# Expert weights loaded into tiles that the attention leaves, a third buffer of bucket rows, and the first experts' rows turned on TensorE

## The chip, the core and the metric

The kernel runs on one core of a Trainium2 chip. The metric is the device time of one execution in microseconds (us), median of several runs. Of the engines, PE is TensorE (matmuls), DVE is VectorE, ACT is ScalarE, POOL is GpSimd, and SP is SyncE, which here only issues DMAs. DMAs issued by SP stand in the profile under queue q1 (hardware_dynamic), those issued by POOL under q0 (software_dynamic); 16 DMA engines work for both.

## What is computed

Blockwise causal attention over 8 batches, 8 heads, 576 positions, 64 channels; its output, as 4608 rows of 512, goes through a noisy top-2 router and a mixture of 8 experts (512 to 1024 to 512, ReLU between).

```python
scores = np.where(mask, scale * q @ k^T, -1e9); attn = softmax(scores); x = (attn @ v) as (4608, 512)
noisy = x @ w_gate + log1p(exp(x @ w_noise)) * noise
top2 = the two largest of noisy per row; top2_w = softmax over these two
for e in range(8):
    for k in range(2):
        mask = top2[:, k] == e
        h = np.maximum(x[mask] @ w1[e], 0.0)
        out[mask] += top2_w[mask, k, None] * (h @ w2[e])
```

## The kernel before

**Stages.** The batches go in four groups of two (g = 0 to 3, 1152 rows each). For each group POOL loads q, k and v, PE turns q and k into `qT` and `kT`, computes scores, ACT takes the exponentials into `esc` (two buffers, one per half of the heads), PE multiplies by v (`vt`), DVE divides and writes the rows into `xr`. Then the router: PE turns the rows of `xr` (five pieces; their copies out of PSUM land in three buffers `xT0` to `xT2`), computes the logits from them (`logits`, L596), and DVE makes slots. POOL scatters the rows by `slots` into a bucketed DRAM tensor `xd` (18 indirect DMAs for each group, `scatter`, L707).

**Buckets.** Groups 0 and 1 form half 0, groups 2 and 3 half 1. In each half each expert has a bucket of 640 rows: 16 buckets, b = 0 to 15, where b is half times 8 plus expert. For a bucket SP loads the rows with a transposing DMA from `xd` into `xg` (`load_x`, L840; two buffers `xg0`, `xg1`); PE runs layer 1 (`layer1`, L898, matmul at L906: 64 matmuls of 128x320), ACT the ReLU into `h` (L912), PE layer 2 (`layer2`, L916, matmul at L922: five row tiles of eight matmuls of 128x512). The result rows go through `y` tiles to the DRAM tensor `yd` (`store_row`, L935, on SP). Buckets 0 and 1 are cut finer: pieces of 256, 256 and 128 rows, of which the first needs group 0's scatters alone; part of them is worked on between the attention of group 3. In the second half POOL gathers from `yd` (L945), DVE sums (L958, L980), and the rows are stored to the output.

**Weights.** Each expert has four pieces, W1 in two and W2 in two (`load_w`, L815), cast from float32 to bfloat16 by DMAs that POOL issues. Experts 0 and 1 have tiles of their own. Expert 7 lies where the raw q and k lay. Experts 2 to 6 lie in a pool `late`, opened where the attention's tiles lay, and their loads depend on the end of the whole attention (`att_done`).

**What sets the order.** A planner (`Plan`) gives each operation a name, engine costs, a due time, and resources that it takes and frees (buffers, PSUM banks); it simulates and writes the instructions of each engine out in the order that results. The engines work in order. `DUE` spaces the buckets' due times from 150. Operations added with `anchor=True` (weights among them) also wait, on the chip, for the last exponential or ReLU on ACT that stands before them in the plan. Names: `LX` is a load of bucket rows, `F1` and `F2` the layers, `RE` the ReLU, `YS` the store to `yd`, `W1`/`W2` weights, `D3.j` the scatters of group 3.

## Time and profile before

| | us |
|---|---|
| median of three runs (480.6 to 489.99) | 485.77 |
| profiled execution, device time | 478.8 |
| its span, first to last instruction | 477.0 |
| PE busy in the span | 411.8 (86%) |
| ACT busy | 258.9 (54%) |
| POOL busy | 258.6 (54%) |
| DVE busy | 160.2 (34%) |
| q0 (POOL's DMAs), share of 16 engines | 65.7% |
| q1 (SP's DMAs), share of 16 engines | 27.2% |
| mean granted clock of PE | 0.95 |

The profile is of one execution. Its busy shares are averages over stages of different kinds: the attention lasts to about 165 us, the buckets from then to the end. A timeline row gives an instruction's start and how long it took; in square brackets stands the idle time of its engine just ahead of it and what ended it. A row of SP's queue gives the time in which SP was busy issuing, not the transfer. The clock of PE is given as a share of full speed.

### The profile page before, as it was taken

The page shows a single profiled execution, that of the slowest core. Times are in us where ns is not written, and L with a number is a line of the kernel's source. Part 1 is how long each engine was busy: PE and PEld are TensorE (multiplying, and loading weights), DVE is VectorE, ACT ScalarE, POOL GpSimd, SP SyncE. Part 2 cuts the span into 40 slices and gives each one's busy share as a digit, 9 for nine tenths or more (in the row PEclk, how much of TensorE's full clock was granted, in tenths as well). Part 3 has the DMA queues.
Part 4 walks back from the last instruction along what each step waited for, and adds up shares of the span by engine and source line. Part 5 has one row for each costly group of instructions (what it writes and reads, how often), then busy time and mean ns, then how long its engine had stood idle before and what let it go on. Part 6 is the DMA issues. An engine that isn't in the chain of part 4 may idle for free. (4 is left out here: it accounts for less than half of the span.)

```text
span 477.0 us, 10736 instructions
## 1 busy us (share of the span) xinstructions
PE 411.8 (86%) x4308; PEld 262.6 (55%) x4344; DVE 160.2 (34%) x428; ACT 258.9 (54%) x448; POOL 258.6 (54%) x293
## 2 busy tenths in 40 slices
PE   3889999878699898599996989999989939999990
PEld 2567767667466775356553555555545525555550
DVE  4748788774733440000000020002432313233221
ACT  1778789854667644255542445466545524556520
POOL 7756458785874782743211000027577757577764
PEclk9979999996889999799998999999999978999997
DMA  9999999999969789959999993238856494875532
GB/s 122 185 201 188 182 180 153 196 182 173 159 140 192 213 160 227 238 135 201 211 186 221 184 172 97 56 84 163 269 125 166 131 146 133 206 189 184 187 104 90
DMA packets 131945, 80.26 MB, mean 168 GB/s; under 512 B 90848, under 2 KB 119853, under 8 KB 131888
## 3 DMA queue, kind: packets, MB, share of 16 engines
q0 software_dynamic: 69856, 52.37, 65.7%
q1 hardware_dynamic: 62032, 27.14, 27.2%
q8 instruction: 36, 0.59, 0.5%
q14 instruction: 21, 0.17, 0.1%
HBM read 71.43 MB, written 35.17 MB: 223 GB/s over the span
## 5 line engine op out<-in xcount | busy, mean ns | idle before, releaser
L906 PEld LDWEIGHTS <-w 128*128 128x128 bf16 x1088 | 105.3, 100 | 74.0 <-issue 28.5
L495 ACT ACTIVATE esc<-sc 128x1024 bf16<-128x1024 f32 x96 | 93.1, 1027 | 25.4 <-PE sc L476 24.7
L922 PEld LDWEIGHTS <-h 128*128 128x128 bf16 x640 | 62.1, 98 | 68.6 <-issue 2.5
L906 PE MATMUL sc<-xg,w 128*128 128x320 bf16 (+2 forms) x544 | 83.9, 294 | 16.6 <-DVE xr L958 7.4
L711 POOL DMA_INDIRECT xd<-xr,slots x72 | 71.7, 996 | 43.8 <-issue 16.4
L906 PE MATMUL bk<-xg,w 128*128 128x320 bf16 (+1 forms) x544 | 88.2, 303 | 7.1 <-DMA xg<-xd 7.1
L922 PE MATMUL bk<-w,h 128*128 128x512 bf16 x350 | 88.7, 382 | 1.8 <-ACT h L912 0.5
L912 ACT ACTIVATE h<-sc 128x320 bf16<-128x320 f32 (+1 forms) x120 | 50.7, 447 | 47.4 <-PE sc L906 34.9
L945 POOL DMA_INDIRECT xr<-yd,slots x36 | 36.6, 1017 | 67.9 <-DMA yd<-xr 56.9
L912 ACT ACTIVATE h<-bk 128x320 bf16<-128x320 f32 (+1 forms) x124 | 55.7, 453 | 31.4 <-PE bk L906 24.6
L922 PE MATMUL sc<-w,h 128*128 128x512 bf16 x254 | 64.8, 379 | 1.0 <-DVE xr L958 0.4
L469 PE MATMUL sc<-qT,kT 64*128 64x512 bf16 (+4 forms) x320 | 39.8, 313 | 7.4 <-ACT esc L495 5.9
L945 POOL DMA_INDIRECT xr<-yd,grow x35 | 35.9, 1026 | 13.2 <-issue 9.8
L873 DVE TENSOR_TENSOR rtmp<-rc,rowid 128x40 f32<-128x40 f32 x1 | 0.2, 225 | 105.6 <-DMA rc<-xd 105.6
L537 PEld LDWEIGHTS <-esc 128*128 128x128 bf16 x640 | 24.0, 100 | 8.9 <-issue 7.2
L556 DVE TENSOR_TENSOR xr<-bk,rden 128x256 bf16<-128x256 f32 x66 | 28.0, 424 | 2.3
L819 POOL DMA_DIRECT2D w<-in_moe_w_dram x16 | 12.4, 781 | 29.0 <-ACT h L912 28.3
L537 PE MATMUL bk<-vt,esc 128*128 128x65 bf16 x584 | 26.4, 198 | 1.7 <-DVE xr L556 0.8
L416 DVE COPY kT<-bk 128x1024 bf16<-128x1024 bf16 (+1 forms) x24 | 24.9, 1039 | 7.1 <-PE bk L395 6.1
L469 PEld LDWEIGHTS <-kT 64*128 64x128 bf16 x320 | 15.5, 97 | 18.8 <-issue 9.7
L964 POOL DMA_INDIRECT out_dram<-xr,trow x17 | 17.3, 1015 | 15.3 <-DVE xr L958 12.3
L476 PE MATMUL sc<-ones_mat,maskA 64*128 64x64 bf16 x256 | 23.6, 197 | 0.8 <-issue 0.8
(164 smaller groups left out, 415.1 us busy)
## 6 DMA issues: line engine op xcount, KB each, us to landing
w<-in_moe_w_dram POOLq DMA_DIRECT2D x32, 512.0 KB
yd<-xr SPq DMA_DIRECT2D x45, 128.0 KB
rq<-in_q_dram POOLq DMA_DIRECT2D x16, 256.0 KB
rk<-in_k_dram POOLq DMA_DIRECT2D x16, 256.0 KB
vt<-in_v_dram POOLq DMA_DIRECT2D x16, 256.0 KB
yd<-y SPq DMA_DIRECT2D x30, 128.0 KB
out_dram<-o SPq DMA_DIRECT2D x18, 128.0 KB
out_dram<-xr SPq DMA_DIRECT2D x18, 128.0 KB
```

What stands on the lines that cost most here:

```text
L416: nc.vector.tensor_copy(o, i)
L469: nc.tensor.matmul(out=sc[:, hf, off:off + z - a], lhsT=kT[sl, c0 + jt * P:c0 + jt * P + P], rhs=qT[sl, c0 + a:c0 + z], start=True, stop=n ...
L476: nc.tensor.matmul(out=sc[:, hf, off:off + 64], lhsT=maskA[sl, :], rhs=ones_mat[sl, 0:64], start=False, stop=True, skip_group_check=True)
L495: return nc.scalar.activation(out=esc_t[i][:, hh, :, piece * 512:(piece + 1) * 512], in_=sc, func=AF.Exp, scale=scale)
L537: nc.tensor.matmul(out=a[:, hh, :], lhsT=esc[:, hh, hf, c:c + P], rhs=vb[:, jt, hf, h, 0:D + 1], start=(jt == 0), stop=(jt == ib))
L556: nc.vector.tensor_tensor(out=xr[:, idx, st * SET * D:(st + 1) * SET * D].rearrange("p (h d) -> p h d", h=SET), in0=a[:, :, 0:D], in1=rden ...
L711: ins = nc.gpsimd.indirect_dma_start(out=xd[half].bitcast(I32), out_offset=bass.IndirectOffsetOnAxis(ap=slots[:, g * TG + idx, i:i + 1], a ...
L906: nc.tensor.matmul(out=hp[:, j * n:(j + 1) * n], lhsT=w1sb[:, db, fb * P:(fb + 1) * P], rhs=xg[:, db, c0:c0 + n], start=(db == 0), stop=(d ...
L912: return nc.scalar.activation(out=h_t[pl.slot(("h", b))][:, s * nb:(s + 1) * nb, c0:c0 + n], in_=bank(("hp", b, i, s))[:, 0:nb * n].rearra ...
L922: nc.tensor.matmul(out=yp, lhsT=h[:, fb, c * P:(c + 1) * P], rhs=w2sb[:, fb, :], start=(fb == 0), stop=(fb == FB - 1))
L945: ins = nc.gpsimd.indirect_dma_start(out=g_t[pl.slot(key)], out_offset=None, in_=yd[half][0:len(es) * CAP, :], in_offset=bass.IndirectOffs ...
L964: ins = nc.gpsimd.indirect_dma_start(out=out, out_offset=bass.IndirectOffsetOnAxis(ap=trow[:, e, c:c + 1], axis=0), in_=out_tile(("o", b, ...
```

## The change

- `NX` stays at two `xg` buffers, and the three `xT` buffers become one tile, whose memory is a third `xg` buffer once the last logits (`G3.0` to `G3.4`) are read.
- The buckets' due times start at 135, not 150.
- The pool `late` goes. Expert 2 lies where the raw q and k lay; experts 3 and 4 in `esc0` and `esc1`; expert 5 in `vt0` and `vt1`; expert 6 in `qT` and `kT`; expert 7 in the rest of `esc0` and `esc1`. Each load depends on those parts of the attention that read that tile last (`freed`), and the weights are issued in the order of the experts.
- The rows of buckets 0 and 1 are loaded in tiles of 128 rows with plain DMAs into `y` tiles (`load_tile`); PE turns each with four transposes into a PSUM bank (`XT`), and DVE or ACT copies it into `xg` (`XX`). There are two more `y` tiles, one of them the tile `zero`, after its use.
- The scatters of group 3 have a later due time (190).

```diff
-    NG_, NY, NO, NX = 0, 3, 0, 2
+    NG_, NY, NO, NX = 0, 4, 0, 2
-    xT_t = [low.tile([P, 2, DB, P], BF16, name=f"xT{i}") for i in range(3)]
+    xT_all = low.tile([P, 3, 2, DB, P], BF16, name="xT")
+    xT_t = [xT_all[:, i] for i in range(3)]
...
+    xg_t.append(xT_all.rearrange("p a b c d -> p (a b c d)")[:, 0:DB * CAP].rearrange("p (b n) -> p b n", b=DB))
+    zero = consts.tile([P, DR], BF16)
+    y_t += [zero[:, 0:Dm]]
+    pl.resource("y", 1, float("inf"))
...
-                   deps=[f"R{g}.rows", f"R{g}.w1", f"R{g}.tok", f"Z{half}"], due=r1 + 7 + j * 0.9 - 0.,
+                   due=(r1 + 7 - 0. if g < NG - 1 else 190.) + j * 0.9,
...
-    DUE, t_ = {}, 150.
+    DUE, t_ = {}, 135.
-    W1 = {0: ("low", 0), 1: ("low", 1), E - 1: ("rgt", 0)}
-    for e in range(2, E - 1):
-        W1[e] = ("late", e - 2)
...
     def w_of(e, which):
+        if e < EARLY:
+            return (w1_t if which == 1 else w2_t)[e]
+        if e == EARLY:
+            return rgt2()["w1" if which == 1 else "w2"]
+        esc = [esc_t[pl.slot(("esc", last, st))].rearrange("p a b c -> p (a b c)") for st in range(2)]
+        if e < EARLY + 3:
+            return view(esc[e - EARLY - 1], which - 1, which)
+        if e == EARLY + 3:
+            return view(vt[pl.slot(("vt", last - 2 + which))].rearrange("p j b h d -> p (j b h d)"), 0, which)
+        if e == EARLY + 4:
+            return view(qT if which == 1 else kT, 0, which)
+        return view(esc[which - 1], 2, which)
+
+    def freed(e, which):
+        av_done = [[f"A{last}.{st}.{i}" for i in range(TG)] for st in range(2)]
+        if e < EARLY:
+            return []
+        if e == EARLY:
+            return raw_done
+        if e < EARLY + 3:
+            return av_done[e - EARLY - 1]
+        if e == EARLY + 3:
+            return [f"A{last - 1}.{st}.{i}" for st in range(2) for i in range(TG)] if which == 1 else av_done[0] + av_done[1]
+        if e == EARLY + 4:
+            return [f"Q{last}.{u}" for u in range(UG)]
+        return av_done[which - 1]
...
-    w_rel = {0: 60., 1: 100.}
+    w_rel = {0: 60., 1: 100., 2: 140.}
...
+    def load_tile(b, c):
+        half, e = SEQ[b]
+        r = e * CAP + c * P
+        ins = nc.sync.dma_start(out=y_t[pl.slot(("xl", b, c))], in_=xd[half][r:r + P, 0:Dm])
+        return rows_landed(ins, half, groups(b, c // 2))
+
+    def turn_tile(b, c):
+        tp = bank(("xp", b, c)).bitcast(BF16)
+        for db in range(DB):
+            nc.tensor.transpose(tp[:, db * P:(db + 1) * P], y_t[pl.slot(("xl", b, c))][:, db * P:(db + 1) * P], ident)
+
+    def tile_turned(b, c, eng):
+        o = xg_of(b)[:, :, c * P:(c + 1) * P]
+        if eng == "DVE":
+            nc.vector.tensor_copy(o, tp)
+        else:
+            nc.scalar.activation(out=o, in_=tp, func=AF.Copy)
...
+    grant("zeros", ["Z0", "Z1"], (("y", NY, NY + 1),))
+    pl.resource("xg", 1, float("inf"))
+    grant("logits", [f"G{NG - 1}.{j}" for j in range(5)], (("xg", NX, NX + 1),))
```

The order of the instructions changes in two places above all. On SP, before the change, from the load of the last 256 rows of bucket 1 that wait for group 1 (`xg1`) to the load of bucket 4 (the second `xg0` of 640 rows):

```order
L844 DMA_TRANSPOSE xg1_112<-xd0 128x4x256
L938 DMA yd0<-y0_115 128x512
L844 DMA_TRANSPOSE xg1_112<-xd0 128x4x128
L938 DMA yd0<-y1_116 128x512
L938 DMA yd0<-y2_117 128x512
L938 DMA yd0<-y0_115 128x512
L938 DMA yd0<-y1_116 128x512
L938 DMA yd0<-y2_117 128x512
L844 DMA_TRANSPOSE xg0_111<-xd0 128x4x640
L938 DMA yd0<-xr0_106 128x512 x3
L844 DMA_TRANSPOSE xg1_112<-xd0 128x4x640
L938 DMA yd0<-xr0_106 128x512 x2
```

After the change, on SP, from the last but one plain load of bucket 1 (`y2`) to the load of bucket 4 (`xg1`):

```order
L868 DMA y2_115<-xd0 128x512
L868 DMA y3_116<-xd0 128x512
L860 DMA_TRANSPOSE xT_108<-xd0 128x4x640
L975 DMA yd0<-zero_159 128x512
L975 DMA yd0<-y0_113 128x512
L868 DMA y2_115<-xd0 128x512
L975 DMA yd0<-y1_114 128x512
L975 DMA yd0<-xr0_106 128x512 x3
L860 DMA_TRANSPOSE xg0_109<-xd0 128x4x640
L975 DMA yd0<-xr0_106 128x512 x2
L975 DMA yd0<-zero_159 128x512
L860 DMA_TRANSPOSE xg1_110<-xd0 128x4x640
```

The load of bucket 2 stood behind six stores of buckets 0 and 1 and went into `xg0`; it now stands ahead of all of them and goes into `xT`. The loads of buckets 3 and 4 go into `xg0` and `xg1`.

On POOL, before the change, from the scatters of group 2 (`xd1` from `xr0`) past those of group 3 (`xr1`):

```order
L711 DMA xd1<-xr0_106,slots_101 9728x260 x18
L817 DMA w1_2_3612<-in_moe_w1_dram 128x2x1024 x2
L819 DMA w2_2_3617<-in_moe_w2_dram 128x4x512 x2
L817 DMA w1_3_3613<-in_moe_w1_dram 128x2x1024 x2
L711 DMA xd1<-xr1_107,slots_101 9728x260 x18
L819 DMA w2_3_3618<-in_moe_w2_dram 128x4x512 x2
L817 DMA w1_4_3614<-in_moe_w1_dram 128x2x1024 x2
```

After the change, on POOL, the same place:

```order
L716 DMA xd1<-xr0_106,slots_101 9728x260 x18
L836 DMA w1_2_3617<-in_moe_w1_dram 128x2x1024 x2
L838 DMA w2_2_3618<-in_moe_w2_dram 128x4x512 x2
L836 DMA esc0_139<-in_moe_w1_dram 128x2x1024 x2
L838 DMA esc0_139<-in_moe_w2_dram 128x4x512 x2
L836 DMA esc1_140<-in_moe_w1_dram 128x2x1024 x2
L838 DMA esc1_140<-in_moe_w2_dram 128x4x512 x2
L716 DMA xd1<-xr1_107,slots_101 9728x260 x12
L836 DMA vt0_143<-in_moe_w1_dram 128x2x1024
L716 DMA xd1<-xr1_107,slots_101 9728x260 x2
```

Six weight pieces stood between the scatters of groups 2 and 3; now twelve stand there, and the last scatters of group 3 are mixed with the pieces of expert 5.

## Rows read from the trace of the kernel before

**Rows 1.** Timeline of PE: start, us, engine, line, op, tiles, shape, count [idle before].

```profile
196.12 1.23 PE L906 MATMUL bk<-xg,w 128*128 128x320 bf16 x4 [7.13 <-DMA xg<-xd]
197.14 1.27 PE L906 MATMUL sc<-xg,w 128*128 128x320 bf16 x4
198.20 2.30 PE L906 MATMUL bk<-xg,w 128*128 128x320 bf16 x8
200.34 1.79 PE L906 MATMUL sc<-xg,w 128*128 128x320 bf16 x12
...
255.15 1.23 PE L906 MATMUL sc<-xg,w 128*128 128x320 bf16 x4 [5.42 <-DMA xg<-xd]
...
258.66 0.71 PE L906 MATMUL sc<-xg,w 128*128 128x320 bf16 x4
...
275.73 0.70 PE L906 MATMUL sc<-xg,w 128*128 128x320 bf16 x4 [1.54 <-DMA xg<-xd]
...
293.20 0.71 PE L906 MATMUL sc<-xg,w 128*128 128x320 bf16 x4
...
311.13 0.71 PE L906 MATMUL sc<-xg,w 128*128 128x320 bf16 x4
...
392.90 1.23 PE L906 MATMUL sc<-xg,w 128*128 128x320 bf16 x4 [7.37 <-DVE xr L958]
```

**Rows 2.** Timeline of PE around the router of group 3 and after it.

```profile
164.53 0.39 PE L582 MATMUL bk<-ident,xr 128*128 128x128 bf16 x4
164.76 1.03 PE L922 MATMUL sc<-w,h 128*128 128x512 bf16 x4
165.62 0.45 PE L600 MATMUL sc<-wgn,xT 128*128 128x16 bf16 x12
...
174.39 2.82 PE L906 MATMUL sc<-xg,w 128*128 128x128 bf16 x40
```

**Rows 3.** Timeline of SP's queue: loads of buckets 2, 4, 5 and 6.

```profile
176.37 15.12 SPq L844 DMA_TRANSPOSE xg<-xd  x1
...
210.50 2.39 SPq L844 DMA_TRANSPOSE xg<-xd  x1
...
227.83 13.41 SPq L844 DMA_TRANSPOSE xg<-xd  x1
...
247.80 21.11 SPq L844 DMA_TRANSPOSE xg<-xd  x1
```

**Rows 4.** DMA queues from 212 to 216 us: packets, MB, share of 16 engines.

```profile
q1 hardware_dynamic: 2488, 0.64, 72.2%
```

**Rows 5.** DMA queues from 232 to 255 us.

```profile
q0 software_dynamic: 2707, 3.71, 92.0%
q1 hardware_dynamic: 2686, 0.75, 26.4%
```

**Rows 6.** Stretches: us, busy PE, PEld, DVE, ACT, POOL; clock, DMA share, GB/s.

```profile
164.00:168.00 4.00, 3.95 (x52) 2.92 (x51) 1.82 (x6) 1.75 (x6) 3.08 (x4) 1.00 0.44 152
...
196.00:200.00 4.00, 3.88 (x15) 2.22 (x15) 0.00 (x0) 1.30 (x3) 3.09 (x4) 0.50 1.51 308
...
208.00:212.00 4.00, 4.00 (x27) 2.44 (x25) 0.00 (x0) 2.40 (x6) 0.76 (x1) 1.00 0.03 7
...
236.00:240.00 4.00, 3.95 (x22) 2.08 (x22) 0.00 (x0) 1.59 (x4) 0.74 (x1) 1.00 1.15 201
```

**Rows 7.** Timeline of POOL: first weights, last of six landed, last scatter.

```profile
168.56 1.55 POOL L817 DMA_DIRECT2D w<-in_moe_w_dram  x2
...
191.85 0.97 POOL L711 DMA_INDIRECT xd<-xr,slots  x1 [1.39 <-DMA w<-in_moe_w_dram]
...
204.66 0.98 POOL L711 DMA_INDIRECT xd<-xr,slots  x1 [0.30 <-issue]
```

**Rows 8.** Timeline of ACT: one copy of turned rows out of PSUM.

```profile
165.01 0.60 ACT L591 ACTIVATE xT<-bk 128x512 bf16<-128x512 bf16 x1 [0.49 <-ACT y L931]
```

**Rows 9.** Timeline of POOL: the first gather of the second half.

```profile
317.99 1.07 POOL L945 DMA_INDIRECT xr<-yd,slots  x1 [56.58 <-DMA yd<-xr]
```

More of the change, by code (lines that the diff above doesn't have):

```diff
@@ L761 @@
             pl.add(f"D{g}.{j}", {"POOL": 1.28}, lambda e, g=g, j=j: scatter(g, j),
-                   deps=[f"R{g}.rows", f"R{g}.w1", f"R{g}.tok", f"Z{half}"], due=r1 + 7 + j * 0.9 - 0.,
-                   free=[("xr", g)], dma=0.36)
+                   deps=[f"R{g}.rows", f"R{g}.w1", f"R{g}.tok", f"Z{half}"],
+                   due=(r1 + 7 - 0. if g < NG - 1 else 190.) + j * 0.9,
+                   free=[("xr", g)], dma=0.36, after=[] if (g, j) == (NG - 1, 0) else [])
         for n in (f"X{g}.{j}" for j in range(5)):
@@ L901, in layer1 @@
         nb = step_of(b, i)
-        hp, w1sb, xg = bank(("hp", b, i, s)), w_of(e, 1), xg_t[pl.slot(("xg", b))]
+        hp, w1sb, xg = bank(("hp", b, i, s)), w_of(e, 1), xg_of(b)
         for j in range(nb):
@@ L1002 @@
         d0, nb = DUE[(b, i)], step_of(b, i)
[L1003 to L1006 removed]
+        if b < EARLY:
+            for c in range(c0 // P, (c0 + n) // P):
+                pl.add(f"LX{b}.{c}", {"SP": 0.4}, lambda x, b=b, c=c: load_tile(b, c),
+                       deps=rows_of(groups(b, c // 2)), due=d0 - 8 + c * 0.2, take=[("y", ("xl", b, c))], dma=0.6)
+                pl.add(f"XT{b}.{c}", {"PE": 0.24}, lambda x, b=b, c=c: turn_tile(b, c), deps=[f"LX{b}.{c}"],
+                       due=d0 - 3, take=[("bk", ("xp", b, c), 1)], free=[("xl", b, c)], lat=0.25)
+                pl.add(f"XX{b}.{c}", {"DVE": 0.45, "ACT": 0.6}, lambda x, b=b, c=c: tile_turned(b, c, x),
+                       deps=[f"XT{b}.{c}"], due=d0 - 2, free=[("xp", b, c)], lat=0.2,
+                       take=[("xg", ("xg", b))] if c == 0 else [])
+                if c:
+                    pl.ops[f"XX{b}.{c}"].deps.append(f"XX{b}.0")
+        elif i == 0:
+            pl.add(f"LX{b}.0", {"SP": 2.6}, lambda x, b=b: load_x(b),
+                   deps=rows_of([2 * half, 2 * half + 1]), due=d0 - 8, take=[("xg", ("xg", b))],
+                   dma=4.0, seq="xg")
         for st in range(FB // nb):
             d1 = d0 + st * nb * 0.55 * n / NW
[L1009 removed]
+            deps = [f"XX{b}.{c}" for c in range(c0 // P, (c0 + n) // P)] if b < EARLY else [f"LX{b}.0"]
+            deps = deps + [f"W1.{e}.{p}" for p in range(2)]
             pl.add(f"F1.{b}.{i}.{st}", {"PE": nb * max(0.545 * n / NW, 0.23)},
@@ L1204 @@
     marks = sorted((o.end, o.name) for o in pl.order if o.on == "ACT" and (o.name[0] == "S" or o.name[:2] == "RE"))
-    anchors = {}
+    anchors, given = {}, {}
     for o in pl.order:
         got = o.fn(o.on)
+        given[o.name] = got
+        for n in o.after:
+            tc.add_manual_dep(got.ins, given[n].ins.name, SYNC_DEP, reason="leaves the DMA engines to the one before")
         if o.on == "ACT" and (o.name[0] == "S" or o.name[:2] == "RE"):
```

58 lines of the change are left out of this document (20 added, 38 removed).

## The prediction

> **What bounds the kernel now.** I read the chain of work that ended last first; it holds only the last store to the output, so the bound has to be read from the engines. The waits of PE and PE's timeline show it. From about 189 us to the end PE runs buckets 2 to 15 back to back, and a bucket without a stall takes 17.47 us (first layer-1 row of bucket 6 at 275.73, of bucket 7 at 293.20) [rows 1]. Bucket 8 begins at 311.13. PE is the bound of this stage, and what a change can win there is PE's idle time and what follows it. Three holes wait for bucket rows, the DMA transpose into `xg`: 7.13 us before bucket 2 (from 188.99 to 196.12), 5.42 before bucket 5 (to 255.15), 1.54 before bucket 6 (to 275.73) [rows 1]. A fourth, 7.37 us to 392.90, waits for DVE in the second half [rows 1]; the change touches nothing there.
>
> A long hole costs more than its length: at 196 to 200 the granted clock is 0.50, the lower of PE's two levels (1.2 and 2.4 GHz), after PE stood still [rows 6]. After 196.12, 16 matmuls of 128x320 take 4.22 us (to 200.34). At full speed twelve of them show 1.79 us with the overlap of the last, about 0.136 each, so 2.18 was due and 2.04 is lost [rows 1]. After 255.15, eight of these and four of layer 2 take 3.51 us to 258.66 where 1.95 is due (1.09 and 0.86, the latter from 164.76 to 165.62), so 1.56 is lost [rows 1, 2]. The sum is 7.13 + 2.04 + 5.42 + 1.56 + 1.54 = 17.7 us. The cross-check: from 188.99 to 311.13 are 122.1 us; six buckets of 17.47 are 104.8; the difference is 17.3.
>
> Why the rows are late is seen on SP's queue and in the DMA's share. The load of bucket 2 is issued at 176.37, when the last layer-1 piece of bucket 0 (in the row at 174.39) has left its `xg` buffer; those of buckets 5 and 6 at 227.83 and 247.80, again when a buffer is left [rows 2, 3]. From issue to first use they take 19.8, 27.3 and 27.9 us [rows 1, 3]. With few weights beside it the same load is fast: issued at 210.50, almost all its packets (2488 on SP's queue) moved within 212 to 216 us [rows 3, 4]. Beside weights, 2686 of SP's packets took 23 us against 2707 of POOL's [rows 5]. So the packets of the two queues pass about one for one, and 27.9 us is longer than the 26 us that two buffers give (a bucket and a half). The 16 engines are full at 236 to 240, yet stand nearly empty at 208 to 212 [rows 6].
>
> **The change, part by part.**
>
> *Third buffer.* Bucket b now loads into a buffer that bucket b-3 leaves: the lead grows by a bucket, from 26 to 43 us. For bucket 2 the buffer is the router's `xT`, free when the last logits of group 3 are read (165.62 + 0.45 = 166.1) [rows 2], ten microseconds before 176.37. On SP it stands behind loads of bucket 1 only, whose tiles PE turns well before that. Weights for expert 2 are issued from 168.56 as before [rows 7], so the load has 2.5 us and the start-up of those weights nearly to itself; at 164 to 168 the DMA share is 0.44 [rows 6]. It lands between 171 (5 us, as at 210.50) and 194 (27.9 us). I take about 175, for the row at 210.50 is nearest. PE wants it at 188.99 + 2.3 = 191.3 (below). So the 7.13 hole goes. Buckets 5 and 6 have 43 us of lead against 27.9: these holes go too.
>
> *What is late next.* Bucket 3. Its load is issued when bucket 0's last piece ends, 176.4 before and nine turns of 0.23 later now, 178.5, and inside a longer run of weights: POOL issues twelve pieces (experts 2 to 4) ahead of the last scatters, where it issued six. At 27.9 us it lands at 206.4. PE wants it one bucket after 191.3, less the 0.9 of a layer-2 piece that is not between: 207.9. This is nearly a draw. The lower bound is no wait. The upper: if it gets through only when all twelve pieces have landed. Six took from 168.56 to 191.85, 3.9 us each [rows 7]; twelve end at 215, a wait of 7 us and 2 of slow clock. I take 1 us, nearer to the measured load than to the bound.
>
> By the Trainium skill, "DMA: Bandwidth & Descriptors", section "Queues, rings and completion order", each DMA engine takes turns between the queues that have work, packet by packet. By that rule the load lands at about 206 and not at 215; the counts of 2686 and 2707 agree with it.
>
> *Weights earlier, into `esc`, `vt`, `qT`, `kT`.* No bytes are added. The pieces of experts 3 and 4 fill the empty stretch at 204 to 212. In the plan those of expert 5 are tied to the last ReLU of bucket 3 (about 221), expert 6 and the first half of 7 to the end of bucket 4's layer 1 (about 238). Four pieces at 3.9 take 16 us: expert 5 is in at 237, wanted at 243; 6 and 7 by 270, wanted at 260 and 277; expert 6, being first, by 254. Worth nothing by themselves; without that margin each would cost what it is late.
>
> *Scatters behind weights.* POOL's 18 scatters of group 3 ended at 205.6 (last issued at 204.66) [rows 7] and now end near 235, some behind expert 5's pieces. Behind them wait only the record load and bucket 8's rows, wanted past 290. The cover is 50 us: nothing.
>
> *First rows plain, turned by PE.* Six transposes into `xg` go (the 1280 rows of the first two buckets); ten loads of 128 rows and ten turns of four 128x128 come. Four such turns take 0.23 us up to PE's next row (164.53 to 164.76), 0.39 with the overlap [rows 2]. Ten: 2.3 to 3.9; I take 2.3, as other matmuls follow each. The ten copies out of PSUM are split between DVE and ACT; one of the same size is 0.60 us on ACT [rows 8]. PE has other pieces between a turn and its use, so nothing; without that cover, 6 us. Loads: the transposes there had long landed before use, so no gain on PE.
>
> The page "VectorE: DVE Perf Modes" of the Trainium skill, section "The three transpose paths", gives 390 ns for one 128x128 transpose on TensorE. By it the ten tiles cost an estimated 15.6 us. The rows have 0.39 us for four, and the measurement decides.
>
> **The sum.** 17.7 - 2.3 - 1.0 = 14.4 us. The profiled execution took 478.8, so 464.4 in its terms. The runs shown have a median of 485.77, 7.0 above it; I carry the gain over: 485.8 - 14.4 = 471.4, say 471. The second half moves rigidly: POOL waits 56.58 us for the last stores of half 0 before its first gather at 317.99 [rows 9], and its later order is nearly the same.
>
> **The rivals.** (1) *The load of bucket 2 is not earlier*: SP is held at a load of bucket 1, or `xT` is freed late. Then the first hole stays, the others go: 17.7 - 9.2 - 2.3 = 6.2, so 480. For it: SP works in order, and ten more loads stand ahead. Against: their tiles are turned by 160. (2) *Weights crowd out rows a bucket later*: bucket 3 waits 7 + 2, perhaps bucket 7 again by some: gain 5 to 6, 480. For it: the engines are full to the last [rows 6]. Against: the one-for-one passing. (3) *Slower*: the same crowding already strikes bucket 2. If its load does not get through before expert 2's pieces and lands behind all twelve, at 215, PE waits 24 us there and 2 of clock: 17.7 - 2.3 - 26 = -10.6, so 496. It decides from a landing at 206. Against: no load here took over 27.9 us, and that gives 194. (4) *More*: the runs shown lose more than the profiled one, perhaps in these same holes, since these hang on DMA; then up to 22, 464. (5) *A turn costs PE 1.56 us*, each of its transposes standing alone at what four took: 15.6 in all, gain 1.1, 485; spoken against by 0.23 for four. By the page's 390 ns this is the time.
>
> **Chances.** Forecast (466 to 476) 0.62; (1) 0.10; (2) 0.09; (3) 0.08; (4) 0.08; (5) 0.03. A measurement of this kernel tells about 2% from no change, so faster begins below 476. Faster takes the forecast less its upper edge and (4): 0.66. Same takes (1), (2), (5) and that edge: 0.26. Slower is (3): 0.08. To keep 8 in 10 the range runs from 462, in (4), to 482, past (1) and (2). The likeliest case has 466 to 476 for itself.
>
> **What would show it.** In the trace after: the load of bucket 2 issued near 166 and no hole before bucket 2; bucket 2 beginning at 190 to 192 and bucket 8 at 295 to 298; a hole of 0 to 2 us before bucket 3, none before 5 and 6; ten turns of about 0.25 to 0.4 us each. Wrong would be: a wait of PE for `w`, `esc` or `vt`; a hole before bucket 3 over 5 us; or bucket 8 early and the end not, which would put the loss in the second half.

## The result, and the profile after

The changed kernel takes 454.34 us (median of four runs, 449.30 to 461.84) where the kernel before, in the same series, takes 483.19 (479.18 to 489.99). The ratio is 0.935, 95% interval 0.918 to 0.952: faster, by 28.9 us in the medians. The prediction was 471 us in a range of 462 to 482: the direction was right, the gain twice the 14.4 us forecast, and the time lies below the range. Ratios leave out executions more than 1.5% above the quickest of their kernel, medians keep them.

The profiled execution of the changed kernel has a span of 455.0 us against 477.0. The first part of its page (busy us, share of the span, instructions) answers to the table of before:

```profile
span 455.0 us, 11018 instructions
...
PE 408.5 (90%) x4351; PEld 261.9 (58%) x4384; DVE 162.5 (36%) x435; ACT 263.2 (58%) x451; POOL 260.2 (57%) x293
```

Of the 22 us, PE was busy for 3.3 less (411.8 before) and idle for 18.7 less. The timeline of PE in the changed kernel, at a turn and at the starts of buckets 2, 4 to 6, 8, 12 and 13, shows where; it answers to [rows 1, 2]:

```profile
163.84 0.39 PE L874 MATMUL sc<-ident,y 128*128 128x128 bf16 x4
164.07 1.03 PE L959 MATMUL bk<-w,h 128*128 128x512 bf16 x4
...
187.79 0.71 PE L943 MATMUL sc<-xT,w 128*128 128x320 bf16 x4
...
223.59 0.71 PE L943 MATMUL bk<-xg,esc 128*128 128x320 bf16 x4
...
240.92 0.43 PE L943 MATMUL sc<-xT,vt 128*128 128x320 bf16 x2
241.81 0.45 PE L943 MATMUL sc<-xT,vt 128*128 128x320 bf16 x2 [0.46 <-DMA vt<-in_moe_w_dram]
...
252.18 1.87 PE L959 MATMUL sc<-vt,h 128*128 128x512 bf16 x4 [3.33 <-DMA vt<-in_moe_w_dram]
...
265.62 0.71 PE L943 MATMUL sc<-xg,qT 128*128 128x320 bf16 x4
...
300.28 0.71 PE L943 MATMUL sc<-xT,w 128*128 128x320 bf16 x4
...
371.30 0.71 PE L943 MATMUL bk<-xg,esc 128*128 128x320 bf16 x4
...
388.63 0.71 PE L943 MATMUL sc<-xg,vt 128*128 128x320 bf16 x4
```

No row at the start of a bucket has an idle time for `xg` any more. Bucket 5 has a new wait, for the weights of expert 5 in `vt`: it takes 24.7 us from its first row to that of bucket 6, where bucket 4 takes 17.33. And bucket 12, which took 27.5 us before with the hole of 7.37 [rows 1], takes 17.33. SP's queue shows the loads of buckets 2 and 3, issued at 163 and 177 where the first was issued at 176.37 [rows 3]:

```profile
162.97 3.19 SPq L860 DMA_TRANSPOSE xT<-xd  x1
...
177.30 15.42 SPq L860 DMA_TRANSPOSE xg<-xd  x1
```

POOL's timeline shows when the pieces of expert 5 (`vt`) were issued:

```profile
220.21 0.75 POOL L836 DMA_DIRECT2D vt<-in_moe_w_dram  x1 [0.35 <-ACT h L949]
...
227.08 0.77 POOL L836 DMA_DIRECT2D vt<-in_moe_w_dram  x1 [3.49 <-ACT h L949]
...
230.46 0.83 POOL L838 DMA_DIRECT2D vt<-in_moe_w_dram  x1
...
234.33 0.80 POOL L838 DMA_DIRECT2D vt<-in_moe_w_dram  x1 [0.45 <-ACT h L949]
```

The row of the stretch in which PE waits for them has the clock at 0.83 in the mean (columns as in [rows 6]):

```profile
240.00:260.00 20.00, 16.07 (x80) 8.49 (x79) 0.00 (x0) 7.78 (x18) 5.09 (x7) 0.83 1.23 192
```

By stage, from the starts of buckets 2 and 8 and the span, the first pair of profiles compares with the forecast like this (forecast: 4.8 = 196.12 - 191.3; then 2.04 of slow clock, 8.52 of buckets 5 and 6, less 1.0):

| | before | after | gained | forecast |
|---|---|---|---|---|
| start of bucket 2 | 196.1 | 187.8 | 8.3 | 4.8 |
| bucket 2 to bucket 8 | 115.0 | 112.5 | 2.5 | 9.6 |
| bucket 8 to the end of the span | 165.9 | 154.8 | 11.1 | 0 |

So the gain was missed in the second half, where the change edits nothing, and the bucket stage gave less than forecast. Bucket 12 alone is 10.2 us shorter (27.5 and 17.3), nearly all of the 11.1.

### The profile page after: what moved, and what is told of

The parts are those of the page before. It is cut to its first block, busy times and chain, and to the rows that moved or that the text cites. A ratio compares the mean times of both kernels' runs of the same rounds, so it can differ in the third digit from the quotient of the medians.

```text
span 455.0 us, 11018 instructions
## 1 busy us (share of the span) xinstructions
PE 408.5 (90%) x4351; PEld 261.9 (58%) x4384; DVE 162.5 (36%) x435; ACT 263.2 (58%) x451; POOL 260.2 (57%) x293
## 5 line engine op out<-in xcount | busy, mean ns | idle before, releaser
L716 POOL DMA_INDIRECT xd<-xr,slots x72 | 72.1, 1001 | 48.3 <-DMA esc<-in_moe_w_dram 19.4
L949 ACT ACTIVATE h<-sc 128x320 bf16<-128x320 f32 (+1 forms) x126 | 55.1, 447 | 28.2 <-PE sc L943 17.4
L949 ACT ACTIVATE h<-bk 128x320 bf16<-128x320 f32 (+1 forms) x118 | 53.2, 454 | 18.0 <-PE bk L943 11.3
L943 PEld LDWEIGHTS <-w 128*128 128x128 bf16 x448 | 40.8, 98 | 15.9 <-issue 1.8
L943 PEld LDWEIGHTS <-esc 128*128 128x128 bf16 x384 | 37.6, 98 | 17.8 <-issue 0.3
L959 PE MATMUL bk<-w,h 128*128 128x512 bf16 x150 | 37.3, 379 | 0.9 <-ACT h L949 0.5
L959 PE MATMUL sc<-esc,h 128*128 128x512 bf16 x122 | 30.2, 379 | 0.6 <-ACT xr L966 0.3
L542 PEld LDWEIGHTS <-esc 128*128 128x128 bf16 x640 | 24.1, 100 | 8.9 <-issue 7.6
L542 PE MATMUL bk<-vt,esc 128*128 128x65 bf16 x584 | 26.5, 198 | 2.4 <-DVE kT L421 0.6
L959 PE MATMUL bk<-esc,h 128*128 128x512 bf16 x106 | 26.6, 379 | 0.4
L943 PE MATMUL sc<-xg,esc 128*128 128x320 bf16 x168 | 26.7, 299 | 0.1
L943 PE MATMUL bk<-xg,esc 128*128 128x320 bf16 x152 | 24.2, 299 | 0.0
```

The costliest lines, as they stand in the source:

```text
L542: nc.tensor.matmul(out=a[:, hh, :], lhsT=esc[:, hh, hf, c:c + P], rhs=vb[:, jt, hf, h, 0:D + 1], start=(jt == 0), stop=(jt == ib))
L716: ins = nc.gpsimd.indirect_dma_start(out=xd[half].bitcast(I32), out_offset=bass.IndirectOffsetOnAxis(ap=slots[:, g * TG + idx, i:i + 1], a ...
L943: nc.tensor.matmul(out=hp[:, j * n:(j + 1) * n], lhsT=w1sb[:, db, fb * P:(fb + 1) * P], rhs=xg[:, db, c0:c0 + n], start=(db == 0), stop=(d ...
L949: return nc.scalar.activation(out=h_t[pl.slot(("h", b))][:, s * nb:(s + 1) * nb, c0:c0 + n], in_=bank(("hp", b, i, s))[:, 0:nb * n].rearra ...
L959: nc.tensor.matmul(out=yp, lhsT=h[:, fb, c * P:(c + 1) * P], rhs=w2sb[:, fb, :], start=(fb == 0), stop=(fb == FB - 1))
```

## The experiments

Each series timed its kernels beside the kernel before on one chip, and ratios are to it. In two of the five series the kernel before took 552 and 556 us, since PE and ACT stood still at many places with nothing released to them; a difference of some microseconds can't be read from those.

### Both kernels again, and two parts alone

`before_again` and `after_again` are unchanged. `plain_only` is the kernel before with the plain loads and the turns (`load_tile`, `turn_tile`, `tile_turned`, the two more `y` tiles). `third_only` is the kernel before with the third buffer:

```diff
+    xg_t.append(xT_all.rearrange("p a b c d -> p (a b c d)")[:, 0:DB * CAP].rearrange("p (b n) -> p b n", b=DB))
+    pl.resource("xg", 1, float("inf"))
+    grant("logits", [f"G{NG - 1}.{j}" for j in range(5)], (("xg", NX, NX + 1),))
```

> The kernel before once more, unchanged. Two things that the profile of before showed stand open, since the profile of after has neither: (i) group 3's scores started at 120.1 us after a PE idle of 1.8 at 109.6 and a stretch of granted clock 0.50 at 112 to 120 (after: 114.7), and (ii) PE stood 7.37 us ahead of bucket 12 at 392.9. Theory A (both belong to the kernel): scores of group 3 at 119 to 121 again, a hole of 5 to 9 us in buckets 10 to 13 again, span 475 to 482. Theory B (both were slow DMA of that one execution): scores near 115, no hole over 2 us behind bucket 8, span 460 to 468. The holes before buckets 2 and 5 (7.1 and 5.4) come again under either.

> The changed kernel once more, unchanged, timed. Theory A (its new wait for expert 5's first weights is the kernel's own): PE waits 3 to 4 us at the head of bucket 5, whose length from first to last layer-1 start is about 24.7 us against 17.3 without stall, then the clock at 0.5 for some microseconds; ratio 0.92 to 0.95. Theory B (a slow DMA of that execution): bucket 5 takes under 19 us, and the span is some 6 us shorter, near 448.

> The kernel before with one part of the change: rows of buckets 0 and 1 loaded plainly and turned on TensorE (and the two more y tiles that it needs). Two xg buffers and weights as before. Theory A (the transposing DMAs of 256 rows near 100 us held up the attention of group 3): the scores of group 3 start 4 to 5 us earlier, near 115; the ten turns cost 2.3; the holes before buckets 2, 5 and 6 stay: 2 to 3 us faster than before, ratio 0.993 to 0.997. Theory B (the early stretch was chance): no gain, the turns cost 2.3: ratio 1.003 to 1.008. Rival C: the transposing DMAs cost much more than shown, in the attention and in spread: ratio 0.98 or below.

> The kernel before with one part of the change: the third xg buffer in the memory of xT. Rows of the first buckets by transposing DMA and weights as before. Theory A (the prediction's: the third buffer carries the gain and the weights nothing): the holes before buckets 2, 5 and 6 go, 17.7 us, and no wait for weights comes: ratio 0.96 to 0.966. Rival B (weights set the pace as soon as rows do not: those of experts 3 to 6 land too late in the old placement): the holes turn into waits for w of about half their length: ratio 0.975 to 0.99. Rival C (this is all of the measured gain): ratio 0.93 to 0.945.

The kernel before took 555.5 us (13 runs), 70 more than the first median. The timeline of PE in `before_again` shows such a standstill:

```profile
485.94 1.23 PE L906 MATMUL bk<-xg,w 128*128 128x320 bf16 x4 [8.08 <-issue]
```

Ratios: `after_again` 0.983 (0.976 to 0.991), `plain_only` 1.009 (1.003 to 1.015), `third_only` 0.989 (0.980 to 0.997). What follows is one thing: where the engines stand still by themselves for tens of microseconds, the 29 us between the medians shrink to 13 (542.5 and 555.5). Which holes belong to the kernel this series can't tell; only that bucket 5 took 17.7 us in `after_again`, without a wait for `vt`, against theory A there.

### Parts undone

`after_b` is the changed kernel. `no_plain` loads the first buckets' rows by the transposing DMA again; `two_xg` drops the third buffer; `w5_early` issues the weights of expert 5 sooner:

`no_plain` (and no `XT`, `XX`, `LX` by tiles):

```diff
+            pl.add(f"LX{b}.{i}", {"SP": 1.4}, lambda x, b=b, i=i: load_piece(b, i),
+                   deps=rows_of(groups(b, i)), due=d0 - 8, take=[("xg", ("xg", b))] if i == 0 else [],
...
+        ins = nc.sync.dma_start_transpose(out=xg_of(b)[:, :, c0:c0 + n], in_=xd[half][r:r + n, 0:Dm])
```

`two_xg`:

```diff
-    pl.resource("xg", 1, float("inf"))
-    grant("logits", [f"G{NG - 1}.{j}" for j in range(5)], (("xg", NX, NX + 1),))
```

`w5_early` (in `due` and `rel` of the weights):

```diff
-bucket_due(b0) - 26
+bucket_due(b0) - (41 if e == 5 else 26)
...
-bucket_due(b0) - 45
+bucket_due(b0) - (60 if e == 5 else 45)
```

> The changed kernel a third time, as the reference for the runs beside it. In the first pair of profiles the change took 22 us off (ratio 0.935 in the timed runs); in the second, where PE and ACT stood still again and again with nothing released to them (PE's issue waits up to 8.1 us, 553 us in all for the kernel before), its ratio was 0.983. Theory A (the gain belongs to holes for rows, and the standstills cover or swamp it): where the kernel before is again near 480, the ratio is 0.93 to 0.95; where it is again near 555, 0.975 to 0.99. Theory B (the first ratio was chance): 0.97 to 0.985 at either speed.

> The changed kernel with one part undone: the rows of buckets 0 and 1 come by the transposing DMA again, in pieces of 256, 256 and 128 rows, and PE turns none. Third buffer and weights as in the changed kernel. Theory A (the prediction's: ten turns cost PE 2.3 us and the plain loads win nothing): 2 us faster than the changed kernel, ratio 0.995 of it. Theory B (the plain loads freed the attention of group 3, 4 to 5 us): the scores of group 3 start 4 to 5 us later again, and the kernel is 2 to 4 us slower than the changed one, ratio 1.005 to 1.01 of it.

> The changed kernel with one part undone: two xg buffers, not three. Weights and plain loads as changed. The load of bucket 2 is then issued again when bucket 0's last piece ends, now behind twelve weight pieces. Theory A (the prediction's price of the third buffer, 17.7 us, or more since more weights stand ahead): a hole before bucket 2 of 9 to 20 us and holes before buckets 5 and 6, 18 to 30 us slower than the changed kernel, ratio 1.04 to 1.065 of it. Theory B (the early weights carried the gain, the third buffer little): under 8 us slower, ratio below 1.018.

> The changed kernel with the four weight pieces of expert 5 released 15 us earlier in the plan: they are issued right behind those of expert 4, ahead of the last 16 scatters of group 3, and nothing else moves on PE, DVE or ACT. In the first profile of the changed kernel PE waited 0.5 and 3.3 us for these weights in bucket 5, which then took 24.7 us against 17.3. Theory A (the late issue of expert 5 makes this wait): bucket 5 takes 17.3 to 18 us, and the kernel is 5 to 7 us faster than the changed one at the fast speed (ratio 0.985 to 0.99 of it), 0 to 3 at the slow speed, where no such wait showed. Theory B (crowding: the same bytes only press out the rows of buckets 3 to 5): the wait moves to xg before bucket 4 or 5 and nothing is won, ratio 0.997 to 1.01.

The kernel before took 482.8 us (13 runs). `after_b`: 455.9, ratio 0.951 (0.937 to 0.965), so the gain is real: 27 us. Its profile has a span of 449.4 us; bucket 2 begins at 187.79 as in the first profile, bucket 8 here:

```profile
293.31 0.71 PE L943 MATMUL sc<-xT,w 128*128 128x320 bf16 x4
```

`two_xg`: 475.3, ratio 0.988 (0.983 to 0.994); the third buffer is worth 19.4 us of the changed kernel, where the prediction gave it 17.7. In its timeline of PE there are holes again, other than those of before: a longer one before bucket 2, none before bucket 5, one before bucket 6:

```profile
203.06 1.23 PE L943 MATMUL bk<-xg,w 128*128 128x320 bf16 x4 [12.93 <-DMA xg<-xd]
...
277.85 1.07 PE L943 MATMUL sc<-xg,qT 128*128 128x320 bf16 x4 [3.94 <-DMA xg<-xd]
```

Its load of bucket 2, issued among twelve weight pieces, was there by 203.06, 26.2 us later. Beside six pieces it had been 19.8 [rows 1, 3]; but it did not land behind all twelve, as rival (3) had it, for POOL waited for one of them to land until 206.93. From 184 to 204 us the packets of the two queues (packets, MB, share of 16 engines) passed one for one:

```profile
176.89 14.08 SPq L860 DMA_TRANSPOSE xg<-xd  x1
...
206.93 0.98 POOL L716 DMA_INDIRECT xd<-xr,slots  x1 [2.86 <-DMA esc<-in_moe_w_dram]
...
q0 software_dynamic: 2526, 3.10, 90.5%
q1 hardware_dynamic: 2533, 0.78, 29.3%
```

The Trainium skill says as much ("DMA: Bandwidth & Descriptors", section "Queues, rings and completion order": a DMA engine takes turns between its queues by packet), and these rows agree.

`w5_early`: 458.7, ratio 0.959 (0.946 to 0.971), nothing won. Bucket 5 takes 17.73 us and PE no longer waits for `vt`, but its timeline has a wait for rows one bucket earlier:

```profile
224.06 0.70 PE L943 MATMUL bk<-xg,esc 128*128 128x320 bf16 x4 [3.01 <-DMA xg<-xd]
```

`no_plain`: 470.7, ratio 0.982 (0.969 to 0.995), 14.8 us slower than `after_b`. Both theories missed by far: one said 2 us faster, the other 2 to 4 slower. What theory B said of group 3 came: its scores start at 119.8 us, 4.4 later than in `after_b` (115.4). Yet bucket 2 starts only 1.2 us later (188.95 and 187.79). The rest lies further on: PE waits 7.05 for expert 5's second layer (bucket 5 takes 25.9 us), and bucket 12 has the hole again (26.5):

```profile
260.64 3.21 PE L966 MATMUL sc<-vt,h 128*128 128x512 bf16 x8 [7.05 <-DMA vt<-in_moe_w_dram]
...
385.14 2.29 PE L950 MATMUL sc<-xg,esc 128*128 128x320 bf16 x8 [6.69 <-DVE xr L1002]
```

### The hole in bucket 12

The expectations call it the hole before bucket 12; it lies inside that bucket, whose first row in the kernel before stands at 382.87. What PE waits for there is a PSUM bank, which DVE frees; DVE, in order, waits for the second gather of sum 10 (row tile 10 of half 0). The timelines of POOL, SP and DVE in the kernel before:

```profile
379.41 1.00 POOL L945 DMA_INDIRECT xr<-yd,slots  x1 [0.30 <-issue]
379.64 4.57 SPq L844 DMA_TRANSPOSE xg<-xd  x1
...
391.01 0.75 DVE L981 SCALAR_TENSOR_TENSOR xr<-xr,wts,xr 128x512 f32<-128x512 bf16 x1 [8.74 <-DMA xr<-yd,slots]
```

The same three in the changed kernel:

```profile
366.01 1.00 POOL L982 DMA_INDIRECT xr<-yd,slots  x1 [0.30 <-issue]
367.18 3.30 SPq L860 DMA_TRANSPOSE xT<-xd  x1
...
370.18 0.75 DVE L1018 SCALAR_TENSOR_TENSOR xr<-xr,wts,xr 128x512 f32<-128x512 bf16 x1 [2.17 <-DMA xr<-yd,slots]
```

In both the planned order of POOL, SP and DVE around this place is the same. Before, the load of a later bucket's rows was issued 0.23 us after POOL began on the gather, and the gather was used 11.6 us later; after, the load came 1.17 us behind and the gather was used after 4.2. So the theory: a load issued while the gather is still being issued meets its packets. Four kernels test it. Two hold the load until sum 10 is done (`before_lx13_late`, `no_plain_lx14_late`), one tries to bring it closer (`after_lx14_early`), and `third_only_b` is the third buffer alone again:

`before_lx13_late` (for bucket 13) and `no_plain_lx14_late` (for bucket 14):

```diff
-deps=rows_of(groups(b, i)), due=d0 - 8,
+deps=rows_of(groups(b, i)) + (["SO.10"] if b == 13 else []), due=d0 - 8,
...
-deps=rows_of([2 * half, 2 * half + 1]), due=d0 - 8,
+deps=rows_of([2 * half, 2 * half + 1]) + (["SO.10"] if b == 14 else []), due=d0 - 8,
```

`after_lx14_early`:

```diff
-deps=rows_of([2 * half, 2 * half + 1]), due=d0 - 8,
+deps=rows_of([2 * half, 2 * half + 1]) + (["SO.9"] if b == 14 else []), due=0 if b == 14 else d0 - 8,
```

> The kernel before with one edit: the transposing load of bucket 13 waits until the sum of row tile 10 (DVE) is done, and so stands on SP behind that sum's stores, not ahead of them. In the profile of before it was issued 0.23 us after POOL began to issue the second gather of that sum, the gather landed 11 us later (DVE waited 8.74), and PE stood 7.37 us before bucket 12. In the profile without plain loads the same two were 0.23 apart, and PE stood 6.69; in four others they were 0.95 to 1.4 apart, and PE did not stand. Theory A (the load's packets get ahead of the gather's when it is issued while the gather is still being issued): the gather lands within 4 us, no hole before bucket 12, 7 to 10 us faster than before, ratio 0.979 to 0.986. Theory B (slow memory at that moment, whatever is issued): the hole stays or moves, ratio 0.995 to 1.005.

> The changed kernel without plain loads and turns (first buckets' rows by transposing DMA), and with the transposing load of bucket 14 held until the sum of row tile 10 is done. Theory A (a good half of what plain loads seem to be worth, 14.8 us, is this meeting of a gather and a load, which only follows from how POOL and DVE stand to each other): 7 to 9 us faster than without plain loads alone, ratio to before 0.96 to 0.967, no hole before bucket 12. Theory B (the hole has another cause): ratio 0.978 to 0.985 as without the hold.

> The changed kernel with the transposing load of bucket 14 put one store earlier on SP (between the two stores of sum 9, 0.65 us earlier), so that it is issued about 0.5 us after POOL begins to issue the second gather of sum 10 where it was 1.1 to 1.2. Theory A (load issued inside the gather's issue gets ahead of it): that gather lands 8 to 11 us after its issue, PE stands 5 to 8 us before bucket 12, ratio to before 0.96 to 0.97 where the changed kernel has 0.95. Theory B (0.65 us more or less on SP is nothing): no hole, ratio 0.945 to 0.955.

> The kernel before with the third xg buffer alone, for the second time (the first time PE and ACT stood still at many places for no cause that the profile shows, 553 us for the kernel before, and the ratio was 0.9885). Theory A (the third buffer is worth its 17.7 us, the old placing of weights is no bar, and the meeting of load and gather before bucket 12 stays): ratio 0.96 to 0.968, a hole before bucket 12 of 6 to 8. Rival B (in the old placing the weights set the pace once rows do not): waits for w in buckets 3 to 6, ratio 0.975 to 0.99.

The kernel before took 480.7 us (7 runs). With the load held, the gather is used 4.5 us after its issue in `before_lx13_late`, and PE's idle time is 0.62:

```profile
383.03 1.00 POOL L945 DMA_INDIRECT xr<-yd,slots  x1 [0.30 <-issue]
...
387.52 0.75 DVE L981 SCALAR_TENSOR_TENSOR xr<-xr,wts,xr 128x512 f32<-128x512 bf16 x1 [1.71 <-DMA xr<-yd,slots]
...
389.43 0.70 PE L906 MATMUL sc<-xg,w 128*128 128x320 bf16 x4 [0.62 <-DVE xr L958]
390.16 4.79 SPq L844 DMA_TRANSPOSE xg<-xd  x1
```

Bucket 12 takes 19.8 us instead of 27.5 (PE still waits 1.32 at 393.08). In time less is left: the span is 473.2 us against 477.0 (bucket 2 started 1.3 later, and the rest of the second half lost 2.4). The median is 478.8 against 480.7, short of theory A's 7 to 10, but it is no price: two of the four executions took 474.4 and 475.1, below all seven of the kernel before (480.0 to 487.9), the other two 482.6 and 485.9. `no_plain_lx14_late`: 460.2, ratio 0.953 (0.945 to 0.961), where `no_plain` had 0.982 (0.969 to 0.995); bucket 12 takes 19.0 where it took 26.5, with this idle time of PE in place of 6.69. The wait for expert 5 stays and is longer:

```profile
259.97 3.57 PE L966 MATMUL sc<-vt,h 128*128 128x512 bf16 x8 [9.66 <-DMA vt<-in_moe_w_dram]
...
379.64 1.25 PE L950 MATMUL sc<-xg,esc 128*128 128x320 bf16 x8 [1.35 <-DVE xr L1002]
```

In both kernels the hole goes, as theory A has it, and in the second its time does too: 10.5 us between the medians, of the 15 that plain loads seemed to be worth. `third_only_b`: 464.7, ratio 0.964 (0.957 to 0.971), in theory A's span, with the hole where it was expected:

```profile
368.88 1.00 POOL L947 DMA_INDIRECT xr<-yd,slots  x1 [0.30 <-issue]
368.98 5.28 SPq L846 DMA_TRANSPOSE xT<-xd  x1
...
378.14 0.75 DVE L983 SCALAR_TENSOR_TENSOR xr<-xr,wts,xr 128x512 f32<-128x512 bf16 x1 [4.75 <-DMA xr<-yd,slots]
...
381.37 1.22 PE L908 MATMUL sc<-xg,w 128*128 128x320 bf16 x4 [6.08 <-DVE xr L960]
```

Part of what third buffer and hold leave against the changed kernel shows in ACT's timeline of this run: in bucket 6, which takes 21.8 us, ACT waits for a store of rows (SP issued stores only after a load that held it from 243.02 to 262.14), and PE for ACT, 2.06 us:

```profile
273.55 0.60 ACT L933 ACTIVATE xr<-bk 128x512 bf16<-128x512 f32 x1 [6.62 <-DMA yd<-xr]
```

The changed kernel has two more `y` tiles, and there is no such wait in its bucket 6 (17.33 us). That the tiles are the reason was not tested by themselves.

`after_lx14_early`: 457.3, ratio 0.947 (0.938 to 0.956). The edit didn't bring the two together: the load was issued 0.91 us after the gather, no hole came, and nothing follows for the theory. But this profile too has the wait for expert 5 (1.88 and 2.88 us, bucket 5 takes 24.5).

### Four more, of which little can be read

The next series fell on standstills again (before 551.8 us, 535.7 to 566.4). Two of its kernels were repeated in the last series. The others are `plain_only_b` (as `plain_only`) and `no_plain_lx14_w5` (`no_plain_lx14_late` with the weights of `w5_early`).

> The changed kernel with about 1 us of idle work on POOL (four fills of 128x128 of a tile that is no longer read) put ahead of the first gather of sum 10; nothing else moves. In its profiles the load of bucket 14 was issued 1.13 to 1.17 us after POOL began to issue the second gather of that sum; now it should be 0.0 to 0.25, as in the three kernels that had the hole (0.10 to 0.23). Theory A (a gather whose issue the load cuts into lands behind the load): DVE waits 5 to 9 us for that gather, PE stands 4 to 8 us before bucket 12, ratio to before 0.96 to 0.967 where the changed kernel has 0.935 to 0.95. Theory B (the hole belongs to the kernels with transposed first rows in some other way): no hole, at most 1 us slower, ratio 0.945 to 0.953.

> The kernel before with the third xg buffer alone and the transposing load of bucket 14 held until sum 10 is done. Third buffer alone gave 0.964 of before, with a hole of 6.08 before bucket 12. Theory A (third buffer plus that hole are nearly the whole difference between before and after; weights and plain loads add nothing): 7 to 9 us faster than the third buffer alone, ratio to before 0.945 to 0.952, equal to the changed kernel. Theory B (early weights or plain loads carry a part of their own): 0.96 to 0.965, and the changed kernel stays 5 us or more ahead.

> The kernel before with plain loads and turns alone, for the second time (the first time it stood beside a kernel before of 555 us and had 1.009). Theory A (turns cost 2.3 us, the attention of group 3 gains nothing, and whether load and gather meet before bucket 12 decides the rest): with the meeting ratio 1.0 to 1.008, without it 0.98 to 0.988; the profile tells which by the distance of the two issues (under 0.3 or over 0.9 us). Theory B (plain loads win 15 us by themselves, as undoing them in the changed kernel cost 15): ratio 0.965 to 0.972 whatever the distance.

> The changed kernel without plain loads and turns, with the load of bucket 14 held until sum 10 is done, and with the weights of expert 5 issued right behind those of expert 4. With the first two edits it took 460 us, and its profile had a wait of 9.7 us of PE for expert 5's second layer. Theory A (that wait goes, no turns are paid): 6 to 10 us faster than that, ratio to before 0.933 to 0.942, ahead of the changed kernel by 2 to 8 us. Theory B (the weights then crowd out the rows of buckets 3 and 4, as when this was done in the changed kernel, where nothing was won): ratio 0.948 to 0.957.

Ratios: `after_sg10_later` 0.993 (0.951 to 1.034), `third_lx14_late` 1.013 (0.978 to 1.048), `plain_only_b` 1.038 (0.999 to 1.076), `no_plain_lx14_w5` 1.011 (0.995 to 1.027): intervals wider than what was asked. What plain loads are worth in the kernel before, and whether the wait for expert 5 can be had away together with the turns, stays open.

### The meeting made in the changed kernel, and the hold on the third buffer

`after_sg10_later_b` puts work on POOL ahead of the first gather of sum 10, so that the second one begins closer to the load. `third_lx14_late_b` is the third buffer alone with the load of bucket 14 held as above. The edit of the first (`after_sg10_later` had four fills):

```diff
+    def held_gather(t, i):
+        if (t, i) == (10, 0):
+            for _ in range(3):
+                nc.gpsimd.memset(prem, 0.0)
+        return gather(("sg", t, i), 0, slots[:, t, i:i + 1], range(E))
```

> The kernel before with the third xg buffer alone and the transposing load of bucket 14 held until sum 10 is done, again, since the first time engines stood still all over (before at 552 us) and nothing of some microseconds could be read. Theory A (third buffer plus the hole before bucket 12 are nearly the whole difference of before and after): ratio to before 0.945 to 0.952. Theory B (early weights or plain loads carry a part of their own): 0.96 to 0.965. Where before is again near 550, this stays open.

> The changed kernel with three fills on POOL (some 0.9 us) ahead of the first gather of sum 10, so that the load of bucket 14 is issued 0.1 to 0.3 us after the second gather, as in the kernels with the hole. Theory A (the two meet, gather and load both go slowly): DVE waits 5 to 9 us, PE stands 4 to 8 us before bucket 12, ratio to before 0.955 to 0.967. Theory B (the hole needs more than this distance): no hole, ratio 0.945 to 0.953. In the run with four fills, where engines stood still all over, the distance was 0.32 and the gather landed in 4.2 us, which speaks for B.

The kernel before took 482.8 us (7 runs). The timelines of `after_sg10_later_b`:

```profile
360.81 1.00 POOL L982 DMA_INDIRECT xr<-yd,slots  x1 [0.30 <-issue]
361.08 6.33 SPq L860 DMA_TRANSPOSE xT<-xd  x1
...
368.26 0.75 DVE L1018 SCALAR_TENSOR_TENSOR xr<-xr,wts,xr 128x512 f32<-128x512 bf16 x1 [4.37 <-DMA xr<-yd,slots]
...
371.88 0.70 PE L943 MATMUL sc<-xg,esc 128*128 128x320 bf16 x4 [1.84 <-DVE xr L995]
```

The distance is 0.27 us, and the gather is used 7.4 us after its issue instead of 4.2 to 5.2: so the meeting does delay it. But PE's idle time is 1.84, bucket 12 takes 19.3 us, and the kernel 451.9 (ratio 0.941, 0.931 to 0.951): theory A's hole of 4 to 8 did not come, and the time is theory B's (0.945 to 0.953) within its interval. The run with four fills had a distance of 0.32 and a use after 4.5, against theory A too. The distance alone is thus not enough for the whole hole.

`third_lx14_late_b`: the profile has no hole (bucket 12 takes 17.5 us instead of 25.6) and a span 9.4 us below that of `third_only_b`, but the timed median is 463.0 (457.8 to 467.1), ratio 0.965 (0.954 to 0.977), no better than 0.964. Theory A's time did not come, theory B's did: beside the third buffer and this hole, another part of the change carries some of the gain. In the profile it lies in buckets 3 and 6 (19.9 and 21.9 us, where `after_b` has 17.3 and 17.3).

### What the profiles say together

For the second gather of sum 10: from its issue to that of the load, to its use by DVE, PE's idle time before the row that waits for it, and bucket 12 from start to start (executions without standstills):

| kernel | to the load | to its use | PE idle | bucket 12 |
|---|---|---|---|---|
| before | 0.23 | 11.6 | 7.37 | 27.5 |
| no_plain | 0.23 | 10.2 | 6.69 | 26.5 |
| third_only_b | 0.10 | 9.3 | 6.08 | 25.6 |
| after_sg10_later_b | 0.27 | 7.4 | 1.84 | 19.3 |
| after_lx14_early | 0.91 | 4.9 | none over 0.7 | 17.7 |
| two_xg | 0.95 | 4.7 | none over 0.8 | 17.7 |
| after_b, after, w5_early | 1.13 to 1.38 | 4.2 to 5.2 | none over 0.7 | 17.3 to 17.4 |
| held: before_lx13_late, no_plain_lx14_late, third_lx14_late_b | 6.9 to 7.6 | 4.3 to 5.0 | 0.62, 1.35, none | 19.8, 19.0, 17.5 |

All four with 0.3 us or less have a late gather, and no other has. What else belongs to the full hole is POOL's place: the second gather is issued 67.5 to 68.3 us after bucket 8 began in the three with 6 us and more, 66.6 in `after_sg10_later_b`, 66.8 in `after_lx14_early`, 65.7 to 65.9 in `after`, `after_b`, `two_xg` and `w5_early`. Being late is not enough by itself, since with the load held it was 67.0 to 70.4 without a hole. Why POOL comes 1 to 2 us earlier in the kernels with plain loads, the runs don't tell.

## Why the prediction was right, and where it was wrong

**Right: the third buffer.** The load of bucket 2 was issued at 163 and nothing waited for rows; undoing it cost 19.4 us, doing it alone won 16.0 (464.7 against 480.7), against 17.7 in the sum. The stretch from bucket 2 to 8 takes 105.5 us in `after_b`, 9.5 less than before; forecast were 9.6. That this fits so closely is partly luck: bucket 2 takes 18.5 us in both, since two pieces of bucket 1's layer 2 now lie in it, and the 1.0 kept for bucket 3 was not needed. Counted to the start of bucket 8, `after_b` is 17.8 us ahead (293.3 against 311.1) where 14.4 were forecast. Rivals (1), (2) and (3) fell with it: no hole before bucket 3.

**Wrong: the second half.** "The second half moves rigidly", and "the change touches nothing there", is the step that failed. From bucket 8 to the end the changed kernel is 11.1 us shorter, `after_b` 9.8 (156.1 against 165.9), while bucket 12 alone is 10.2 and 10.1 shorter; `no_plain` has 162.9, and 156.8 with the load held. No instruction had to change places for that. The hole at 392.90 [rows 1] was read as DVE's; one step behind DVE stood a gather that had met a load, and this meeting at 0.2 us was gone once the two were 1.2 us apart. That the load takes part in the hole is shown in three kernels, where it went with the load held. That the meeting alone makes it is not: brought about in the changed kernel, it gave 1.84 us. What the hole costs in timed runs is not settled either: the ratio went from 0.982 to 0.953 with the load held in `no_plain`, stayed at 0.964 and 0.965 with the third buffer alone, and has no price in the kernel before.

**Wrong in two of four undisturbed executions (the changed kernel twice, `after_lx14_early`, `after_sg10_later_b`): expert 5.** "expert 5 is in at 237, wanted at 243" priced four pieces of 3.9 us from 221. In the trace they were issued at 220, 227, 230 and 234, since each is tied to a later ReLU of ACT, so that the last had 6.6 us to the first row of bucket 5. Bucket 5 took 24.7 us, 7 more than without the wait. But `after_b` issued them at the same times, to the last at 234.34, and has no wait; nor has `after_sg10_later_b`, while `after_lx14_early` has it. What differs is the DMA. POOL's queue from 231 to 234 us in `after`, then in `after_b`:

```profile
q0 software_dynamic: 64, 0.13, 69.8%
```

```profile
q0 software_dynamic: 270, 0.58, 87.1%
```

In `after` the load of bucket 6, issued at 224.06, was still moving then; in `after_b`, issued at 221.77, it was through. So this too is a transposing load that met a transfer of POOL's, at the edge of 2 us; no edit tested it. The prediction had the wait only as what would prove it wrong ("a wait of PE for `w`, `esc` or `vt`"), with no price.

**Missed: group 3 begins earlier.** A turn takes PE 0.23 us to its next row and 0.39 with the overlap, as forecast, and the turns are paid for: from the row of the last logits to bucket 2 PE takes 25.3 us in the five undisturbed kernels with turns and the third buffer, 21.0 in the four with that buffer and none (some of it work of buckets 0 and 1 that moved there). `after_b`, then `third_only_b`, where bucket 2 begins at 188.40:

```profile
162.45 0.45 PE L605 MATMUL sc<-wgn,xT 128*128 128x16 bf16 x12
```

```profile
167.38 0.45 PE L602 MATMUL sc<-wgn,xT 128*128 128x16 bf16 x12
```

Yet bucket 2 begins at 185.1 to 188.7 in the former and at 185.7 to 189.0 in the latter, for that row comes earlier with plain loads: at 159.8 to 163.3 in six kernels, at 164.7 to 167.9 in the six without; group 3's scores begin at 113.9 to 116.7 and 116.6 to 120.1. The prediction said of the plain loads "so no gain on PE": the attention gained about what the turns cost. That the transposing loads held the attention up follows from these starts alone and was not tested. Rival (5) fell, and with it the 390 ns for one transpose in the page "VectorE: DVE Perf Modes" of the Trainium skill (section "The three transpose paths"), for here 0.39 us is the time of four.

**The range.** It gave 0.08 to more gain than forecast, by rival (4), whose direction was right and whose cause was not: the extra gain came from a hole that the sum had left standing. Its lower edge of 462, less the 10.2 us of bucket 12, would have been an estimated 452, and the measured 454.3 lies above that. A smaller part of the miss is the starting point: the kernel before took 483.2 beside the changed one, where the sum took 485.8.

No kernel tried beats the changed one beyond its interval; 0.941 of `after_sg10_later_b` is the same as its 0.935 and 0.951.

## What to carry to other kernels

Before a hole is called untouched, follow its wait to the transfer behind it, and look whether another queue's transfer was issued within a few tenths of a microsecond: such a hole can go or come when anything ahead of it shifts, so it belongs into the range. Give each transfer that PE needs a lead longer than its longest measured time beside full queues (here 28 us against 26, then 43). And look at two executions: a wait that lies at the edge is in one and not in the other.
